# Block attention with a Fourier mixer and an MLP on one core: V and the next S in one step, q and k turned in separate steps

## The chip, the cores and the metric

The kernel runs on one core of a Trainium2 chip. The metric is the device time of one execution in microseconds (us). A core has five engines that run side by side, each working through its own instructions in order: TensorE (PE, matmuls and transposes into PSUM), VectorE (DVE), ScalarE (ACT), GpSimd (POOL) and SyncE (SP), which here mostly issues DMAs. They wait for each other by semaphores. PSUM holds what matmuls write, until VectorE or ScalarE has read it.

## What is computed

Attention within chunks of 64 tokens (8 batch elements, 8 heads, 576 tokens, head size 64), then per element a Fourier mix over tokens and features, a normalization and an MLP of width 2048, all in float32:

```python
scores = scale * np.matmul(q_c, k_c.transpose(0, 1, 2, 4, 3))
scores = scores - np.max(scores, axis=-1, keepdims=True)
attn = np.exp(scores)
attn = attn / (np.sum(attn, axis=-1, keepdims=True) + 1e-09)
out = np.matmul(attn, v_c)
...
mixed = np.real(np.fft.fft(np.fft.fft(x, axis=1), axis=2)).astype(np.float32)
u = x + mixed
un = (u - mu) / np.sqrt(var + 1e-06)
ch = np.maximum(un @ w_ch1, 0.0) @ w_ch2
return (u + ch).astype(np.float32)
```

The mix needs a whole batch element, so an element's attention must be finished before its mix, and its mix before its MLP.

## The kernel before

**Tiles.** An attention tile is two chunks of 64 tokens, that is 128 rows, of one element (kinds LO and HI), or the middle chunks of two elements (kind RE). Even elements have five tiles, odd ones four, 36 in all. MLP work is done in groups of four tiles; after those of the eight elements comes a ninth group with the RE tiles.

**One attention tile** goes through these parts:

- `att_T`: q and k are turned so that head features lie on partitions. From element 2 on (`n >= first[2]`) VectorE does it with one block transpose each for q and k (L333), both in the same step; for LO tiles POOL then copies one column of qT (L335). Then `load(n + 1)` issues the next tile's q and k on SP, four or eight DMAs each (L192), into single buffers, which must wait until the transposes have read them. In elements 0 and 1 TensorE transposes and ScalarE copies.
- `att_S`: 16 matmul calls of 64x64 write the scores `sc` (L365) into the one two-bank buffer of the pool `ps_a`. A float32 matmul call becomes two matmuls in the trace, so this is 32 of them.
- `softmax`: VectorE takes row maxima (L378) and subtracts them (L380), ScalarE does the exponential (L386), in place in `ex`.
- `att_P`: four 128x128 transposes of `ex` on TensorE (`turn`, L316, into a buffer of the pool `ps_t`, which has two buffers of one bank each), copied by ScalarE to `pT` (L393). These four are called T(ex) below.
- `att_V`: 16 calls of 64x65 (the 65th column of v is one, so that it gives the sum) write `xp` (L407), also into the buffer of `ps_a`. VectorE adds 1e-9, inverts and multiplies (L429 to L431) into `xall`. Then `load_v` issues a later tile's four v DMAs on SP, into a ring of three.

**The MLP.** For the first two groups the up product, and for the first group the down product, are plain loops of 512 columns. From then on both use a scheme with seven half-size products, numbered `o` = 0 to 6, of 128x256 matmuls. In the up product (`up_halves`) they are done for a pair of row blocks `r` = 0, 1; product `o` of one row block takes two calls, that is four matmuls. Each pair has two PSUM tiles per row block, `pa` (products 0, 1, 4) and `pb` (2, 3, 5, 6), and a matmul into such a tile waits until the last reader of that tile is done. Product 0 is copied by ScalarE (L979), product 1 is added by VectorE (L981), product 2 by VectorE (L983), product 3 by VectorE (L985). So product 1 waits for the copy of product 0, and product 3 for the addition of product 2 right before it, with only the other row block's four matmuls between them. In the down product (`down_halves`) a product of one row half takes sixteen matmuls, and the two halves alternate. The weights of the products come as slabs by DMA from memory (`fetch`, tiles `wa` and `wb`), issued on SP between the loads of q, k and v.

Before an MLP group its tiles are normalized (`normed`: for group 1 on ScalarE, L783, else VectorE, L785) and turned with four transposes each (`turned`, L316 again), called T(un) below, copied to `unT` by ScalarE (tiles 0 and 2, and all of the first two groups, L798) or VectorE (the others). They use the same two `ps_t` buffers. So do the Fourier products `z` (two at once, emptied by ScalarE) and `mix`.

**The order.** It is written by hand. `mlp(g)` yields after short pieces of work: in the plain loops after one row block, in `up_halves` after products 1, 3, 5 and 6, in `down_halves` after each product of a row half. After each yield the main loop calls steps of the next element's side work, `attention(b)`, three empty steps (`PAUSE`) and `fourier(b)`. `sizes` tells how many side steps an element has, and the loop spreads them evenly over the MLP pieces. In `attention` before, a tile has four steps: S with the softmax; the turning of the next tile; V of the tile before, with `ready` (which starts the exchange of rows, `shift`, and the sums, `fold`, on POOL); and T(ex). A first loop `attention_early` and `fourier_early` do element 0 with nothing beside it. Beside these, `round_weight` turns the float64 weights into float32 on VectorE and ScalarE in the first part of the run.

Of the kernel before, what the change touches and what calls it, by code (L numbers as in the profile page):

```python
# [16 lines left out]
def kernel(  # L17
# [153 lines left out]
        more_v[:, i * 2 * NJ * DV:(i + 1) * 2 * NJ * DV].rearrange("p (i j d) -> p i j d", i=2, j=NJ) for i in range(2)  # L171
    ]

    def load(n):

        for src, dst, nm, eng in ((q, qs, "q", nc.sync), (k, ks, "k", nc.scalar if n == 0 else nc.sync)):
            if n < first[1]:  # L180
                i = 2 * n + (nm == "k")
                t = start[:, (4 + i) * DM:(5 + i) * DM].rearrange("p (j r d) -> p j (r d)", r=2, d=D)
            else:
                t = one_p.tile([128, NJ, 4 * D], FP32, tag=nm, name=nm)
            if n >= first[2]:
                (b0, c0), (b1, c1) = chunks(n)
                parts = [(0, 32, b0, min(c0, c1))] if b0 == b1 else [(0, 16, b0, c0), (16, 16, b1, c1)]
                for g in range(4):
                    e, x0 = g // 2, g % 2 * 32
                    for r0, rows, b, c in parts:  # L190
                        from_ = src[b, e:H:2, c * CH:c * CH + 4 * rows, :].rearrange("j (p t) d -> p j (t d)", t=4)
                        eng.dma_start(  # L192
                            out=t[32 * g + r0:32 * g + r0 + rows, :, 0:4 * D - 32],
                            in_=from_[:, :, x0:x0 + 4 * D - 32],
                        )
                dst[n] = t
                continue
            t = t.rearrange("p j (r d) -> p (j r) d", d=D)[:, 0:H]
            (b0, c0), (b1, c1) = chunks(n)
            if b0 == b1 and c1 == c0 + 1:  # L200
                parts = [(0, 128, b0, c0)]
            else:
                parts = [(0, CH, b0, c0), (CH, CH, b1, c1)]
            for p0, np_, b, c in parts:
                eng.dma_start(
                    out=t[p0:p0 + np_], in_=src[b, :, c * CH:c * CH + np_, :].rearrange("h p d -> p h d")
                )
            dst[n] = t
# [72 lines left out]
            free.remove(fit[0])  # L281
            nc.sync.dma_start(out=raw(i).rearrange("p f r -> p (f r)"), in_=pieces[i][1].bitcast(U32))

    def round_weight(i):

        if i < len(pieces):
            w, t = pieces[i][0], raw(i)
            lo, hi, wi = t[:, :, 0], t[:, :, 1], w.bitcast(U32)
            p = power[i] = three_p.tile([128, 512], U32, tag="o", name="power")
            nc.vector.tensor_scalar(wi, hi, 0x000FFFFF, None, ALU.bitwise_and)
            nc.scalar.activation(out=w, in_=wi, func=ACTF.Copy, scale=2.0 ** -20, bias=1.0)
            nc.vector.tensor_scalar(p, hi, 0x7FF00000, None, ALU.bitwise_and)
            nc.scalar.activation(out=p, in_=p, func=ACTF.Relu, scale=-1.0, bias=top[:, 0:1])
            nc.scalar.activation(out=p, in_=p, func=ACTF.Relu, scale=-8.0, bias=top[:, 1:2])
        if 0 < i <= len(pieces):  # L300
            w, t = pieces[i - 1][0], raw(i - 1)
            lo, hi = t[:, :, 0], t[:, :, 1]
            p = power.pop(i - 1)
            nc.vector.scalar_tensor_tensor(w, lo, 2.0 ** -52, w, ALU.mult, ALU.add)
            nc.vector.scalar_tensor_tensor(p, hi, 0x80000000, p, ALU.bitwise_and, ALU.bitwise_or)
            nc.vector.tensor_tensor(out=w, in0=w, in1=p.bitcast(FP32), op=ALU.mult)
            r = raws.pop(i - 1)
            if i - 1 + len(spaces) < N_EARLY or r < N_LATE:
                free.append(r)
            load_weight(max(raws, default=i - 1) + 1)  # L310
# [6 lines left out]
        return pt  # L317


    def att_T(n):  # L320

        if n >= first[2]:
            for src, dst, nm in ((qs, qT, "qT"), (ks, kT, "kT")):
                a = src.pop(n).rearrange("p j (t b d) -> p j t b d", t=4, b=2)[:, :, :, 0]
                t = one_p.tile([128, NJ, 2, CH + 1], FP32, tag=nm, name=nm)
                low = kind(n) == LO and nm == "qT"
                to = t[:, :, :, CH:0:-1] if low else t[:, :, :, 0:CH]  # L330
                if kind(n) == HI:
                    to = to[:, :, ::-1]
                nc.vector.transpose(out=to.rearrange("p j c (r t) -> p j t c r", t=4), in_=a)  # L333
                if low:
                    nc.gpsimd.tensor_copy(t[:, :, :, 0:1], t[:, :, :, CH:CH + 1])  # L335
                dst[n] = t.rearrange("p j c t -> p (j c) t")
            if n + 1 < NT:
                load(n + 1)
            return
        a = qs.pop(n)  # L340
        pt = turn(lambda j: a[:, 2 * j:2 * j + 2, :].rearrange("p h d -> p (h d)"))
        t = one_p.tile([128, 2 * NJ, CH + 1], FP32, tag="qT", name="qT")
        low = kind(n) == LO
        nc.scalar.copy(t[:, :, CH:0:-1] if low else t[:, :, 0:CH], pt.rearrange("p j (c t) -> p (j c) t", c=2))
        if low and n < first[1]:
# [28 lines left out]
    def softmax(n):  # L374
        sc = scs.pop(n)
        s4 = sc[:, :, 0:NJ * CH].rearrange("p e (j k) -> p e j k", j=NJ)
        mx = sm_p.tile([128, 2, NJ], FP32, tag="mx", name="mx")
        nc.vector.tensor_reduce(out=mx, in_=s4, axis=AX.X, op=ALU.max)  # L378
        ex = two_p.tile([128, NJ, 2, CH], FP32, tag="ex", name="ex")
        nc.vector.tensor_tensor(  # L380
            out=ex.rearrange("p j e k -> p e j k"),
            in0=s4,
            in1=mx.unsqueeze(3).to_broadcast([128, 2, NJ, CH]),
            op=ALU.subtract,
        )
        nc.scalar.activation(out=ex, in_=ex, func=ACTF.Exp, scale=scale)  # L386
        es[n] = ex

    def att_P(n):
        ex = es.pop(n)  # L390
# [5 lines left out]
    def att_V(n):  # L396
        a, b = pT.pop(n), vs.pop(n)
        if n < first[1]:
            xp = early_xp
        else:  # L400
            xp = ps_a.tile([128, 2, 512], FP32, tag="att", name="xp")
            xp = [xp[:, e] for e in range(2)], xp
# [12 lines left out]
        xo = x[:, DM:0:-1] if kind(n) == HI else x[:, 0:DM]  # L415
        xo = xo.rearrange("p (j e d) -> p e j d", j=NJ, e=2)
        rd = sm_p.tile([128, 2, NJ], FP32, tag="rd", name="rd")
        if n < first[1]:
            for e in range(2):
                nc.vector.tensor_scalar_add(rd[:, e], xp[0][e][:, D:NJ * DV:DV], 1e-9)  # L420
            nc.vector.reciprocal(out=rd, in_=rd)
            for e in range(2):
                xe = xp[0][e][:, 0:NJ * DV].rearrange("p (j d) -> p j d", j=NJ)
                nc.vector.tensor_tensor(
                    out=xo[:, e], in0=xe[:, :, 0:D], in1=rd[:, e].unsqueeze(2).to_broadcast([128, NJ, D]), op=ALU.mult,
                )
# [79 lines left out]
    def attention_early():  # L506
# [32 lines left out]
        keep_warm(3)  # L539
        turn_tables()  # L540
        round_next()
        round_next()

    def attention(b):

# [10 lines left out]
                fold(b, NM)  # L556
            return kind(n) == HI

        if b < 2:
            att_T(lo)  # L560
            yield
        for n in range(lo, hi + 1):
            att_S(n)
            softmax(n)
            yield
            if n + 1 < NT and (b > 0 or n < hi):
                att_T(n + 1)
            yield
            if n > lo:
# [351 lines left out]
    def down_plain(g, h1):  # L921
# [4 lines left out]
        for m in range(KF):  # L926
# [15 lines left out]
                    store(n, o)  # L942
            for j in range(G):
                due = KF - (G - j + 1)
                if m == due - 1:
                    normed(g + 1, j)
                if m == due:
                    turned(g + 1, j)
# [125 lines left out]
    with tc.manual_schedule():  # L1074
# [26 lines left out]
            for _ in range(times):  # L1101
                nc.tensor.matmul(out=idle[:, 0:NQ], lhsT=warm[:, 0:128], rhs=warm[:, 0:NQ], start=True, stop=True)

        def round_next():
            nonlocal n_w
            if n_w <= len(pieces):
                round_weight(n_w)
                n_w += 1

        keep_warm(8)  # L1110
# [2 lines left out]
        for step, _ in enumerate(fourier_early()):  # L1113
            if step == 0:
                turn_dim_tables()
        round_next()
        PAUSE = 3

# [7 lines left out]
        sizes = []  # L1126
        for b in range(1, B):
            n_tiles = first[b + 1] - first[b]
            sizes.append(4 * n_tiles + PAUSE + 2 + NM + b % 2 + (b == 1))
        done, cur = 0, 0  # L1130
        begin = [0]
        for g in range(NG):
# [96 lines left out]
```

## Time and profile before

| What | us |
|---|---|
| median of 3 runs (1121.31 to 1125.09) | 1122.53 |
| the profiled execution, its own time | 1123.98 |
| span of its instructions | 1122.2 |
| matmuls of the scheme's down product with `h`, one row of the page (512, of `pa`) | 116.1 |
| all S matmuls (1152), busy | 25.0 |
| all V matmuls (`xp`, 992), busy | 21.6 |
| T(ex) (144) and T(un) (144), busy | 21.8 and 21.9 |
| block transposes of q and of k (27 each), busy | 29.8 and 29.4 |

The profile has a page (busy time of each engine, the time in slices, the costliest groups) and answers to questions about the trace. Three kinds of lines are used here. A *wait* line reads: engine, tile and line that waited, `<-` what ended the wait, then the total in us, how often, and the longest. A *timeline* line reads: start in us, duration in us, engine, line, operation, tile written `<-` tiles read, shape, how many instructions were merged into the line, and in brackets the engine's idle time before it with what ended it. A *groups* line has busy time and mean duration of all instructions of one kind. Matmuls overlap: the end of one is modelled and lies behind the start of the next, so the distance of starts tells what a matmul costs in a stream.

### The profile page before, as it was taken

How to read it: one execution, taken by the hardware profiler on the slowest of the kernel's cores; microseconds unless marked ns; L12 is line 12 of the kernel's file. 1: busy time of each engine (PE TensorE's matmuls, PEld its weight loads, DVE VectorE, ACT ScalarE, POOL GpSimd, SP SyncE). 2: the span in 40 equal slices, each digit the busy share in tenths (PEclk: the TensorE clock that was granted, in tenths of full speed). 3: DMA queues.
4: the chain of work that ended last, by engine and by line, in shares of the span. 5: the costliest groups of instructions: out<-in, count | busy, mean ns of one | idle time of the engine just before them, and what ended most of it. 6: DMA issues, size and time to landing. Idle time of an engine off the chain costs nothing. (4 is left out here: it accounts for less than half of the span.)

```text
span 1122.2 us, 18759 instructions
## 1 busy us (share of the span) xinstructions
PE 1090.6 (97%) x7042; PEld 845.3 (75%) x7042; DVE 571.0 (51%) x1206; ACT 298.3 (27%) x725; POOL 276.3 (25%) x403
## 2 busy tenths in 40 slices
PE   8899999999999999999999999899999999999998
PEld 6544454446888888788888888778888888888887
DVE  4799987332555365563555355635454434323521
ACT  4688443221112311322122212221132102201210
POOL 4200003235404240063105230154024400130130
PEclk9999999999999999999999999999999999999999
DMA  8777647678475536772567356853654346446332
GB/s 171 226 195 180 158 147 236 179 233 294 149 226 163 160 137 215 213 212 79 177 194 214 114 178 199 226 157 110 194 199 113 113 144 204 141 149 195 89 113 75
DMA packets 147969, 192.72 MB, mean 172 GB/s; under 512 B 66126, under 2 KB 104014, under 8 KB 140712
## 3 DMA queue, kind: packets, MB, share of 16 engines
q1 hardware_dynamic: 145768, 190.46, 56.1%
q8 instruction: 56, 0.92, 0.3%
q0 software_dynamic: 512, 0.68, 0.3%
q10 hardware_dynamic: 1600, 0.39, 0.2%
q14 instruction: 33, 0.27, 0.1%
HBM read 167.22 MB, written 24.12 MB: 171 GB/s over the span
## 5 line engine op out<-in xcount | busy, mean ns | idle before, releaser
L880 POOL TENSOR_TENSOR h<-h 128x256 f32<-128x256 f32 x64 | 55.5, 873 | 412.7 <-PE pb L974 303.5
L1021 PE MATMUL pa<-wb,h 128*128 128x256 f32 x512 | 116.1, 381 | 0.0
L1021 PE MATMUL pb<-wb,h 128*128 128x256 f32 x512 | 115.0, 381 | 0.0
L974 PE MATMUL pb<-unT,wa 128*128 128x256 f32 x448 | 106.6, 381 | 4.1 <-DVE wa L983 4.1
L974 PE MATMUL pb<-wa 128*128 128x256 f32 x448 | 107.3, 382 | 1.1 <-DMA wa<-s 1.1
L974 PE MATMUL pa<-unT,wa 128*128 128x256 f32 x448 | 107.8, 383 | 0.0
L1021 PEld LDWEIGHTS pa<-wb,h 128*128 128x128 f32 x512 | 95.8, 190 | 14.6 <-issue 1.6
L1021 PEld LDWEIGHTS pb<-wb,h 128*128 128x128 f32 x512 | 95.8, 190 | 12.9
L974 PEld LDWEIGHTS pb<-unT,wa 128*128 128x128 f32 x448 | 84.3, 190 | 18.3 <-DVE wa L983 6.8
L974 PEld LDWEIGHTS pb<-wa 128*128 128x128 f32 x448 | 83.4, 190 | 14.3 <-DVE wa L981 1.5
L974 PEld LDWEIGHTS pa<-unT,wa 128*128 128x128 f32 x448 | 83.2, 190 | 11.6
L989 ACT ACTIVATE h<-pa 128x256 f32<-128x256 f32 x56 | 21.5, 383 | 176.1 <-PE pa L974 143.1
L890 PE MATMUL up<-unT,wa 128*128 128x512 f32 x128 | 58.0, 599 | 2.4 <-ACT h L898 1.6
L981 DVE TENSOR_TENSOR wa<-pa,wa 128x256 f32<-128x256 f32 x56 | 23.8, 425 | 70.6 <-PE pa L974 70.6
L928 PE MATMUL dn<-wb,h 128*128 128x512 f32 x128 | 57.7, 599 | 1.3 <-ACT h L898 1.3
L1021 PE MATMUL pa<-wb,yall 128*128 128x256 f32 x256 | 58.2, 382 | 0.0
L974 PE MATMUL pa<-wa 128*128 128x256 f32 x224 | 54.1, 384 | 3.8 <-ACT wa L979 3.8
L907 PE MATMUL up<-unT,wa 128*128 128x512 f32 x128 | 57.5, 598 | 0.0
L1021 PE MATMUL pb<-wb,yall 128*128 128x256 f32 x256 | 57.1, 380 | 0.0
L1021 PE MATMUL pb<-wb 128*128 128x256 f32 x256 | 56.6, 379 | 0.0
L1021 PEld LDWEIGHTS pb<-wb 128*128 128x128 f32 x256 | 48.2, 190 | 6.3
L1021 PEld LDWEIGHTS pa<-wb,yall 128*128 128x128 f32 x256 | 47.7, 190 | 6.9 <-issue 0.5
(233 smaller groups left out, 1646.0 us busy)
## 6 DMA issues: line engine op xcount, KB each, us to landing
wb<-s SPq DMA_DIRECT2D x56, 1024.0 KB
wa<-s SPq DMA_DIRECT2D x196, 256.0 KB
xall<-in_moe_w_ch_dram SPq DMA_DIRECT2D x22, 512.0 KB
q<-in_q_dram SPq DMA_DIRECT2D x96, 112.0 KB
k<-in_k_dram SPq DMA_DIRECT2D x96, 112.0 KB
v<-in_v_dram SPq DMA_DIRECT2D x124, 64.0 KB
yall<-in_moe_w_ch_dram SPq DMA_DIRECT2D x10, 512.0 KB
s<-wb SPq DMA_DIRECT2D x20, 256.0 KB
```

The lines of the kernel that those rows point to most:

```text
L880: nc.gpsimd.tensor_tensor(out=h1[:, m, hi], in0=h1[:, m, lo], in1=h1[:, m, hi], op=ALU.subtract)
L890: nc.tensor.matmul(out=up, lhsT=w1[:, kk, m * 128:(m + 1) * 128], rhs=unT[:, kk], start=(kk == 0), stop=(kk == KD - 1),)
L907: nc.tensor.matmul(out=up, lhsT=w1[:, kk, m * 128:(m + 1) * 128], rhs=unT[:, kk], start=(kk == 0), stop=(kk == KD - 1),)
L928: nc.tensor.matmul(out=dn, lhsT=h1[:, m, s * 128:(s + 1) * 128], rhs=w2[:, m, :], start=(m == 0), stop=(m == KF - 1),)
L974: nc.tensor.matmul(out=dst, lhsT=w[:, kk, r], rhs=rhs[o][:, kk], start=(o in (0, 2) and kk == 0), stop=(kk == 1), skip_group_check=True,)
L981: nc.vector.tensor_tensor(out=b, in0=dst, in1=a, op=ALU.add)
L989: nc.scalar.activation(out=h1[:, m, lo], in_=dst, func=ACTF.Relu)
L1021: nc.tensor.matmul(out=dst, lhsT=lhs[:, m], rhs=w[:, m], start=(o in (0, 2) and m == 0), stop=(m == HF - 1), skip_group_check=True,)
```

## The change

- From element 2 on `attention` has three steps for a tile: the exponential, with turning and loading of the next tile's q; T(ex), with turning and loading of the next tile's k; V, directly followed by S and the softmax's VectorE part of the next tile, and only then `load_v`. The first tile's S is a step of its own. Element 1 keeps its four steps.
- The exponential is a function of its own, called one step after the subtraction.
- From element 2 on V writes into the two buffers of `ps_t`, and its sums and results are read one buffer at a time (five VectorE instructions in place of three).
- `sizes` counts three steps for a tile from element 2 on.
- In the plain down product `normed` of the next group's tiles is called one piece earlier.
- At the start, ScalarE's three operations on the second rounded weight piece are put off until after the copies of the first Fourier product of element 0.

```diff
-    def load(n):
+    def load(n, which="qk"):
         for src, dst, nm, eng in ((q, qs, "q", nc.sync), (k, ks, "k", nc.scalar if n == 0 else nc.sync)):
+            if nm not in which:
+                continue
...
-    def round_weight(i):
+    def round_weight(i, later=None):
...
+            def fraction(w=w, wi=wi):
+                nc.scalar.activation(out=w, in_=wi, func=ACTF.Copy, scale=2.0 ** -20, bias=1.0)
+
+            def exponent(p=p):
+                nc.scalar.activation(out=p, in_=p, func=ACTF.Relu, scale=-1.0, bias=top[:, 0:1])
+                nc.scalar.activation(out=p, in_=p, func=ACTF.Relu, scale=-8.0, bias=top[:, 1:2])
+
             nc.vector.tensor_scalar(wi, hi, 0x000FFFFF, None, ALU.bitwise_and)
-            nc.scalar.activation(out=w, in_=wi, func=ACTF.Copy, scale=2.0 ** -20, bias=1.0)
+            if later is None:
+                fraction()
             nc.vector.tensor_scalar(p, hi, 0x7FF00000, None, ALU.bitwise_and)
-            nc.scalar.activation(out=p, in_=p, func=ACTF.Relu, scale=-1.0, bias=top[:, 0:1])
-            nc.scalar.activation(out=p, in_=p, func=ACTF.Relu, scale=-8.0, bias=top[:, 1:2])
+            if later is None:
+                exponent()
+            else:
+                later += [fraction, exponent]
...
-    def att_T(n):
+    def att_T(n, which="qk"):
         if n >= first[2]:
             for src, dst, nm in ((qs, qT, "qT"), (ks, kT, "kT")):
+                if nm[0] not in which:
+                    continue
...
-                load(n + 1)
+                load(n + 1, which)
...
-        nc.scalar.activation(out=ex, in_=ex, func=ACTF.Exp, scale=scale)
         es[n] = ex
+        if n < first[2]:
+            exponential(n)
+
+    def exponential(n):
+        nc.scalar.activation(out=es[n], in_=es[n], func=ACTF.Exp, scale=scale)
...
             xp = early_xp
+        elif n >= first[2]:
+            xp = [ps_t.tile([128, 512], FP32, tag="pt", name="xp") for _ in range(2)], None
...
-        if n < first[1]:
+        if xp[1] is None:
...
-        round_next()
+        round_next(put_off)
...
-        if b < 2:
-            att_T(lo)
+        if b > 1:
+            att_S(lo)
+            softmax(lo)
             yield
+            for n in range(lo, hi + 1):
+                exponential(n)
+                if n + 1 < NT:
+                    att_T(n + 1, "q")
+                yield
+                att_P(n)
+                if n + 1 < NT:
+                    att_T(n + 1, "k")
+                yield
+                att_V(n)
+                if n < hi:
+                    att_S(n + 1)
+                    softmax(n + 1)
+                if n + 3 < NT:
+                    load_v(n + 3)
+                yield ready(n)
+            return
+        att_T(lo)
+        yield
...
-                if m == due - 1:
+                if m == due - 2:
                     normed(g + 1, j)
...
             if step == 0:
                 turn_dim_tables()
+                for do in put_off:
+                    do()
...
-            sizes.append(4 * n_tiles + PAUSE + 2 + NM + b % 2 + (b == 1))
+            sizes.append((4 * n_tiles + 1 if b == 1 else 3 * n_tiles + 1) + PAUSE + 2 + NM + b % 2)
```

More of the change, by code (lines that the diff above doesn't have):

```diff
@@ L565, in attention @@
             yield
-            if n + 1 < NT and (b > 0 or n < hi):
+            if n + 1 < NT:
                 att_T(n + 1)
@@ L1102, in keep_warm, with round_next @@
                 nc.tensor.matmul(out=idle[:, 0:NQ], lhsT=warm[:, 0:128], rhs=warm[:, 0:NQ], start=True, stop=True)
-        def round_next():
+        put_off = []
+        def round_next(later=None):
             nonlocal n_w
             if n_w <= len(pieces):
-                round_weight(n_w)
+                round_weight(n_w, later)
                 n_w += 1
```

## The prediction

> **What bounds the kernel now.** I read the page's busy shares first, then who waited for whom on TensorE, then the timeline where waits and short matmuls stand.
>
> ```profile
> span 1122.2 us, 18759 instructions
> ...
> PE 1090.6 (97%) x7042; PEld 845.3 (75%) x7042; DVE 571.0 (51%) x1206; ACT 298.3 (27%) x725; POOL 276.3 (25%) x403
> ```
>
> TensorE (PE) is busy 97% of the span at a granted clock of 0.999. So time is won only where PE does needless work or waits. The rows of its waits:
>
> ```profile
> PE pb L974 <- DVE wa L983: 4.1, 4, 1.0
> PE pa L974 <- ACT wa L979: 3.8, 7, 0.5
> ...
> PE pt L316 <- ACT un L783: 1.7, 1, 1.7
> ...
> PE z L604 <- POOL pm L495: 1.7, 1, 1.7
> ```
>
> Total, times, longest. A 128x256 matmul is drawn 0.38 us long, but in a stream the starts are 0.216 us apart (eight between 685.26 and 686.99); a row therefore shows some 0.16 us less than the time lost. I count from start to start. The same view shows a cost that no wait row has:
>
> ```profile
> 668.92 3.62 PE L1021 MATMUL pb<-wb,yall 128*128 128x256 f32 x16
> 672.47 0.70 PE L407 MATMUL xp<-v,pT 64*64 64x65 f32 x32
> 673.10 3.72 PE L1021 MATMUL pb<-wb,yall 128*128 128x256 f32 x16
> 676.66 0.60 PE L316 MATMUL pt<-ident,un 128*128 128x128 f32 x4
> ```
>
> Sixteen matmuls need 16 x 0.2158 = 3.45 us, yet the 64x64 block starts after 3.55 and the transposes after 3.56; the block's own step is 0.63. One block of 64x64 matmuls costs 0.093 + 0.63 + 0.104 = **0.823 us**; the 44 blocks after 290 us all give 0.822 to 0.824. Inside, the records start in groups of four, 0.058 apart (672.580, 672.638, 672.699), so eight groups are 0.467 us of work. The other 0.356 is going into the shape and out again.
>
> Two waits at a pair's start:
>
> ```profile
> 457.01 0.70 PE L365 MATMUL sc<-kT,qT 64*64 64x64 f32 x32
> ...
> 457.64 1.99 PE L974 MATMUL pa<-unT,wa 128*128 128x256 f32 x8
> 457.78 0.69 DVE L378 TENSOR_REDUCE mx<-sc 128x8 f32<-128x512 f32 x1 [0.23 <-PE sc L365]
> 458.50 0.69 DVE L380 TENSOR_TENSOR ex<-sc,mx 128x512 f32<-128x512 f32 x1
> 459.23 0.63 ACT L386 ACTIVATE ex<-ex 128x512 f32<-128x512 f32 x1 [1.02 <-DVE ex L380]
> 459.76 0.63 ACT L979 COPY wa<-pa 128x256 f32<-128x256 f32 x2
> 460.17 1.99 PE L974 MATMUL pa<-wa 128*128 128x256 f32 x8 [0.54 <-ACT wa L979]
> ...
> 462.00 1.89 PE L974 MATMUL pb<-wa 128*128 128x256 f32 x8
> ...
> 462.62 1.10 DVE L333 STREAM_TRANSPOSE qT<-q 128x512 f32<-128x512 f32 x1
> 463.56 1.06 DVE L333 STREAM_TRANSPOSE kT<-k 128x512 f32<-128x512 f32 x1
> 464.47 0.73 DVE L983 TENSOR_TENSOR wa<-pb,wa 128x256 f32<-128x256 f32 x2
> 464.93 1.99 PE L974 MATMUL pb<-unT,wa 128*128 128x256 f32 x8 [1.04 <-DVE wa L983]
> ```
>
> The exponential waits for VectorE (DVE), and the copy of product 0 behind it on ScalarE (ACT) holds product 1: late 0.70 us. Both block transposes stand ahead of product 2's addition, which holds product 3: due at 463.73, started 464.93, late 1.20.
>
> **The change, part by part** (minus is time won).
>
> *V and S in one block.* In the changed issue order 21 S blocks stand directly behind a V block: four for each even batch element from 2 on, three for each odd one. Each pair saves one way in and out: 21 x 0.356 = **-7.5**. A rule speaks against it. The Trainium skill, "TensorE: Matmul & The Clock Gate", in the part on the clock gate under "Wait — 56ns, not 53.3ns?", says that starts of matmuls never come closer than about 25 ns however small they are. By it, 32 matmuls are 0.80 us, the whole 0.823 is work, and the pairing saves nothing. The row decides: starts within a group are 5 to 7 ns apart and a matmul averages 14.6 ns. I take 7.5; zero is the far end.
>
> *Exponential one step later.* It no longer stands between S and product 0. All seven such waits go: 7 x 0.70 = **-4.9**. What follows it, T(ex), still has over two us after VectorE is done: S to T(ex) is at least 6.9 us of PE work, the chain V's reads, reduction, subtraction, exponential some 4.1.
>
> *Transposes and loads of q and k apart.* The four waits of 1.20 go. In six places (three each in elements 4 and 6) the q transpose alone stays between the additions of product 1 and product 2: 463.56, where it would end by these rows, + 0.46 (464.47 to 464.93) = 463.99 against 463.73 due, 0.26 each. -4.8 + 1.6 = **-3.2**. Each transpose issues four or eight 112 KB loads on SP; these now come in two bursts with slab loads (wa<-s) between, where one burst of k loads took 5.34 us at 340.53. Late slabs cost PE 1.4 us in two places; I leave them (0 to -1.4). POOL's copy of column 0 (0.20) moves along and has a step before S. The v loads now stand behind S, which SP does not wait for.
>
> *V's results in the two ps_t buffers.* In six places, once an element, the order is T(un) of the third normed tile, V, S. V's second buffer is the one that T(un) just filled, and it must first be copied by ACT. The nearest row is the last T(un) before the first MLP:
>
> ```profile
> 51.24 0.60 PE L316 MATMUL pt<-ident,un 128*128 128x128 f32 x4
> ...
> 52.51 3.70 PE L890 MATMUL up<-unT,wa 128*128 128x512 f32 x8 [0.67 <-ACT unT L798]
> ```
>
> The four transposes take 0.43, so PE is 0.84 late. V's first matmuls hide about 0.15: 6 x 0.7 = **+4.2** (0.5 to 1.2 each, the more if ACT is busy). Elsewhere the first buffer is long empty.
>
> *VectorE's burst.* V in two buffers gives five reads (the early tile at 28.08: 0.24 for two, 0.20, 0.76 for two), then 0.69 + 0.69 for S. By these starts, V's first matmul + 0.75 + 1.2 + 1.4, the burst ends 3.3 us after V's start, and PE's next dependent product can start at 3.3 + 0.46 = 3.76. Three pairs (elements 3, 5, 7) stand between products 1 and 2 of a pair, where product 3 is due 2.93 after V's start (1.29 - 0.09 + 1.73): 3 x 0.83 = **+2.5**; three lone V there, +0.15. The other 18 stand in the down product, where the other row half gives 3.45 us, or behind products 5 and 6. Here a second rule warns: the skill's "TensorEngine Tiling (Array Packing)", section "PSUM Bottleneck", says that packing speeds TensorE but not the emptying of PSUM, and to use both engines for it. Here VectorE alone empties V and S. By the rule every pair pays, 21 x 0.83 = +17.4; by the rows it is the three without slack.
>
> *Norm of the next tiles a step earlier in the first down product; steps 4n to 3n+1.* The transposes at 178.55 waited 1.9 for ACT's L783, queued behind an exponential. With S a step later and the norm one (3.6 us) earlier: **-1.9**. At 264.47 z waited 1.9 for POOL's fold; PE work between the last V and z grows from 14.3 to 17.9 us: **-1.9**. In odd elements z's halves move closer (1.7 us between); ACT empties both in about 1.3: 0.
>
> *Two rounding steps put off at the start.* ACT's 0.63 + 0.71 + 0.72 leave the queue ahead of z's copies. But VectorE's share of them starts at 40.06 anyway, so this gives 0.2. They now run after 42.66, ahead of the first rstd (44.02), to about 44.7. VectorE waits for that, and of 0.7 the later wait at 47.99 absorbs 0.3: **+0.4** (-0.2 to +0.7).
>
> Sum: -7.5 - 4.9 - 3.2 - 1.9 - 1.9 + 4.2 + 2.5 + 0.15 + 0.4 = **-12.2 us**. The profiled execution took 1123.98 us around its span of 1122.2, 1.45 above the median of 1122.53. It becomes 1111.8, the median **1110.4**.
>
> **Rivals.**
> 1. *New waits eat most of it.* ACT is busy at the six T(un), 1.2 each (+3.0), and the 18 other bursts cost 0.25 each (+4.5): 1118. For: V, S and two transposes make over 4 us of VectorE work per tile. Against: VectorE is 51% busy. 15%.
> 2. *No drain saved*, the issue floor rules or S waits for its own transposes: 1110.4 + 7.5 = 1118. Against: the 14.6 ns. 6%.
> 3. *Slower: every pair runs into VectorE.* Place: all 21. With one 0.42 addition already queued ahead, each costs 1.25: 26.3 instead of 2.5, so +11.6: 1134. It decides from a mean of 0.87 a pair, where the loss passes 3.4 us. Against: the 3.45 us of the down product. 5%.
>
> My forecast has 74%; its own range, from the ends above (slabs 1.4, burst 2.5, T(un) 1.2, start 0.6 below; T(un) 3, transposes 1.6, other bursts 2 above), is 1105 to 1117. Up to 1118 it takes in rivals 1 and 2 as worked out. No change is within 0.3% (1119.2 to 1125.9), about what these runs can tell apart. Faster: 0.74 and about two thirds of rivals 1 and 2, 0.87; same 0.08; slower 0.05.
>
> **What would show it.** In the profile after: V and S within one stretch of about 1.29 us; no wait of pa for ACT's wa; a new wait of xp for ACT's unT, six times; pb's waits for wa three times near 0.8 and six small; the waits at 178 and 264 gone; PE's busy time down by some 7. Wrong if a paired block still costs 1.65, if xp waits over 1 us each, or if PE waits for VectorE in the down product.

## The result, and the profile after

The changed kernel took 1115.60 us, the median of six runs (1114.57 to 1118.42); the kernel before, beside it, 1123.44 (1121.31 to 1125.66). The ratio is **0.9934**, 95% interval 0.9915 to 0.9952. By the medians 7.8 us were won. The profiled execution took 1115.22 us, against 1123.98 before: 8.8 us won, where the prediction added up 12.2. The time lies in the predicted range; the sum was 3.4 us too good.

The head of the page after, and rows of its view of TensorE's waits (microseconds in total, times, longest):

```profile
span 1113.4 us, 18823 instructions
...
PE 1085.2 (97%) x7042; PEld 848.6 (76%) x7042; DVE 582.7 (52%) x1260; ACT 297.7 (27%) x725; POOL 277.7 (25%) x403
```

```profile
PE pb L1017 <- DVE wa L1026: 3.7, 6, 1.2
PE xp L428 <- ACT unT L841: 2.5, 6, 0.4
PE pb L1017 <- DVE h L1034: 2.5, 3, 1.2
...
PE pa L1017 <- ACT wa L1022: 0.7, 2, 0.4
```

PE is busy 5.4 us less than before with as many matmuls (some 7 were expected). The first row holds the predicted waits of product 3, behind VectorE's burst (its five reads of V and two operations on S) and behind a q transposition. The second is the predicted wait of V behind T(un). The third, product 6 waiting for product 5's addition on VectorE, was not in the prediction. The last row shown stands where the seven waits behind the exponential stood; it has two places of another kind.

The timeline of one pair in element 3, PE, VectorE and the first of POOL's work:

```profile
337.09 0.70 PE L428 MATMUL xp<-v,pT 64*64 64x65 f32 x32
337.61 0.65 PE L380 MATMUL sc<-kT,qT 64*64 64x64 f32 x32
...
338.19 1.99 PE L1017 MATMUL pb<-wa 128*128 128x256 f32 x8
...
339.26 1.26 POOL L500 TENSOR_TENSOR sum<-xall 128x512 f32<-128x512 f32 x1 [0.18 <-POOL sum L499]
339.76 0.69 DVE L395 TENSOR_TENSOR ex<-sc,mx 128x512 f32<-128x512 f32 x1
340.37 0.74 DVE L1026 TENSOR_TENSOR wa<-pb,wa 128x256 f32<-128x256 f32 x2
...
340.83 1.99 PE L1017 MATMUL pb<-unT,wa 128*128 128x256 f32 x8 [0.65 <-DVE wa L1026]
...
342.00 0.43 DVE L1028 TENSOR_TENSOR h<-pb,wa 128x256 f32<-128x256 f32 x1 [0.89 <-PE pb L1017]
...
342.34 0.75 DVE L921 TENSOR_TENSOR wb<-h 128x256 f32<-128x256 f32 x1
...
345.09 0.98 DVE L922 TENSOR_TENSOR yall<-wb,h 128x256 f32<-128x256 f32 x1
345.86 1.97 POOL L522 TENSOR_TENSOR pm_rest<-two 64x128 f32<-64x128 f32 x4
346.00 1.07 DVE L348 STREAM_TRANSPOSE qT<-q 128x512 f32<-128x512 f32 x1
346.92 0.73 DVE L1034 TENSOR_TENSOR h<-pb,wa 128x256 f32<-128x256 f32 x2
...
347.38 1.35 PE L1017 MATMUL pb<-wa 128*128 128x256 f32 x5 [1.10 <-DVE h L1034]
```

V starts at 337.09, the burst ends at 340.4, product 3 starts 0.81 late (340.83). So far as predicted. With product 2's additions done at 341.1, VectorE has caught up: it stands idle for 0.89 us until product 3 is there (342.00). In the next five microseconds it falls behind again. The four operand operations of the down product (L921, L922), 0.42 us each where nothing disturbs them, take 0.75 to 0.98 while POOL runs its sums over the tile that has just been finished. A q transpose follows, the addition of product 5 comes behind that, and product 6 is 1.26 late.

From start to start, the terms are these (us; negative is time won against before). "Late" is the time from where the PE stream alone would have started a matmul to where it did.

| term | predicted | measured | where |
|---|---|---|---|
| V and S in one stretch | -7.5 | -7.1 | 15 blocks of 1.29, one of them 0.42 longer; 6 behind T(un) |
| exponential a step later | -4.9 | -3.8 | all seven gone (4.9); two others, 0.53 each |
| q and k transposes apart | -3.2 | -1.7 | 4.8 gone, six new ones of 0.28 to 1.35, 3.13 in all |
| V's second buffer behind T(un) | +4.2 | +4.4 | six blocks of 2.02 in place of 1.29 |
| burst before product 3 | +2.65 | +2.4 | 0.81, 0.82, 0.77 |
| product 6 behind VectorE's work after product 3 | none | +3.0 | 1.26, 1.36, 0.34 |
| first T(un) at 178, z at 264 | -3.8 | -3.8 | both waits gone |
| start, up to the first `up` | +0.4 | +1.0 | z began 1.2 later, behind its loads; from z to `up` -0.2 |
| slab waits | left out | -1.4 | both gone |

The measured column adds up to -7.0. Another 1.3 is that behind a wait or a short stall the second matmul starts 0.1 late too (nine such places fewer after the first T(un) of group 2) and that a wait of `up` at 70 us is 0.4 shorter; the remaining 0.4 or so of the 8.8 I can't place.

By batch element, from the first T(un) of one group to that of the next, a pattern shows that the terms hide. Before, the stretches with the attention of elements 3 to 7 take 119.70, 122.21, 119.48, 122.22, 118.68 us. After: 119.70, 119.30, 119.72, 120.02, 118.66. The odd elements gained nothing.

### The profile page after: what moved, and what is told of

Its sections match the earlier page's. It is cut to its first block, busy times and chain, and to the rows that moved or that the text cites. A ratio compares the mean times of both kernels' runs of the same rounds, so it can differ in the third digit from the quotient of the medians.

```text
span 1113.4 us, 18823 instructions
## 1 busy us (share of the span) xinstructions
PE 1085.2 (97%) x7042; PEld 848.6 (76%) x7042; DVE 582.7 (52%) x1260; ACT 297.7 (27%) x725; POOL 277.7 (25%) x403
## 5 line engine op out<-in xcount | busy, mean ns | idle before, releaser
L1064 PEld LDWEIGHTS pb<-wb,yall 128*128 128x128 f32 x256 | 48.2, 190 | 6.5
```

What stands on the lines that cost most here:

```text
L1064: nc.tensor.matmul(out=dst, lhsT=lhs[:, m], rhs=w[:, m], start=(o in (0, 2) and m == 0), stop=(m == HF - 1), skip_group_check=True,)
```

## The experiments

All times stand beside runs of the kernel before on the same chip (medians 1123.8 to 1124.3), so the ratios to it are compared. The changed kernel's is 0.9934 and its span 1113.4.

**1. V and S apart again, the rest of the change kept.**

```diff
                 att_V(n)
-                if n < hi:
-                    att_S(n + 1)
-                    softmax(n + 1)
                 if n + 3 < NT:
                     load_v(n + 3)
                 yield ready(n)
+                if n < hi:
+                    att_S(n + 1)
+                    softmax(n + 1)
+                    yield
```

The number of steps in an element follows (4n from element 2 on).

> The changed kernel with V and S in separate steps again (four steps a tile), all else kept. Both theories: each of the 21 blocks that were 1.29 us becomes two of 0.823, PE work +7.5 us. Theory A (the pairing pays for itself only partly: it brings the six waits of V for ACT's copy of T(un), 4.4 us, the three waits before product 3 behind V and S on VectorE, 2.4, and those before product 6, 3.0): most of these go, so the time stays within 3 us of the changed kernel, about 1114 to 1118. Theory B (the pairing is the gain, and the waits come from the transposes and the new step count): the waits stay and the time rises by about 7, to 1122.

1119.76 us, ratio 0.9961 (0.9948 to 0.9973), span 1117.5. From element 2 on 53 of its 54 blocks of V or S are 0.82 again (one V behind a T(un) takes 1.55), and no product 3 or 6 is over 0.15 late; three products 1 wait 0.39. So the shape does save 0.36 a pair, and the waits of both products come with the pairing and its places. But the elements are the finding: 3 to 7 take 118.28, 118.40, 118.27, 118.60 and 118.21 us, together **5.6 us less than with the pairs**. What the unpaired kernel loses lies up to the end of element 2's attention: from the first `up` to the first T(un) of group 2, where element 3's stretch begins, it takes 242.3 us, the changed kernel 233.1. There T(ex) waits 5.6 us once, since VectorE, with the softmax in its queue, stands 11.3 us for a transfer:

```profile
PE pt L329 <- ACT ex L406: 5.6, 1, 5.6
```

```profile
246.09 0.58 DVE L922 TENSOR_TENSOR wb<-h 128x256 f32<-128x256 f32 x1 [11.28 <-DMA s<-wb]
```

Behind this wait TensorE's granted clock is 0.50 until 253.7 (see the last section), which costs some 2 us more, and four pairs undone cost 1.4: together about the 9.2.

**2. V in ps_a, S in the two ps_t buffers.**

```diff
-        sc = ps_a.tile([128, 2, 512], FP32, tag="att", name="sc")
+        if n >= first[2]:
+            sc = [ps_t.tile([128, 512], FP32, tag="pt", name="sc") for _ in range(2)]
...
-        elif n >= first[2]:
-            xp = [ps_t.tile([128, 512], FP32, tag="pt", name="xp") for _ in range(2)], None
```

Softmax then takes two reductions and two subtractions of half the width.

> The changed kernel with the PSUM buffers exchanged: V writes into the buffer of ps_a, S into the two of ps_t. Theory A: V starts at once after T(un), and S, 0.5 us later, waits only for the rest of the copy, so the six blocks of 2.02 us become about 1.5: 3 us less, 1112.5. VectorE has the same number of reads, so the waits before products 3 and 6 stay. Rival: the wait only moves from V to S in full (blocks stay at 2.0), or scores in ps_t are read so late (after V's three reads) that the next T(un) or T(ex) waits: no gain, 1115.6 or more.

1118.35 us, ratio 0.9943 (0.9923 to 0.9963), span 1113.5. The six T(un)-V-S blocks shorten from 2.02 to 1.555: the wait is for T(un)'s buffer. But the first S of an element stands directly behind a T(un) as well, and now it waits in V's place:

```profile
PE sc L384 <- ACT unT L854: 2.1, 5, 0.4
```

Five blocks of 1.55 in place of 0.82, +3.6 against -2.8. The expectation had overlooked them.

**3. The exponential back behind the subtraction.**

```diff
         es[n] = ex
-        if n < first[2]:
-            exponential(n)
+        exponential(n)
```

and no call of it in the following step.

> The changed kernel with the exponential directly behind the subtraction again. Five pairs stand directly before a product 0. Theory A: ACT's copy of product 0 queues behind an exponential that waits for V's five reads and the softmax (3.3 us after V's start) and product 1 is late, now more than the 0.70 of before: with the copy of both row blocks some 1.6 us each, 5 times, +8 us, and the waits of pa for ACT's wa grow from 0.7 to about 8: 1123. Rival: the exponential was no matter with pairs, since V's and S's own matmuls cover it: within 2 us of the changed kernel.

1126.56 us, ratio 1.0019 (1.0012 to 1.0027), span 1123.3. The wait row of the page after (0.7, 2) has become

```profile
PE pa L1015 <- ACT wa L1020: 9.8, 9, 1.2
```

11.2 us from start to start. The exponential's later step is worth 10 us once V and S are paired, more than the 4.9 that it took away from the kernel before: with the burst ahead, it waits longer for VectorE and holds ScalarE's copies behind it for as long. Without this step the rest of the change comes out 0.2% behind the kernel before.

**4. q and k transposes and loads in one step.**

```diff
-                    att_T(n + 1, "q")
+                    att_T(n + 1)
                 yield
                 att_P(n)
-                if n + 1 < NT:
-                    att_T(n + 1, "k")
```

> The changed kernel with both block transposes and both loads in the exponential's step again. Theory A: in the six places of elements 4 and 6 between products 1 and 2 the k transpose adds about 1 us to the wait before product 3, and in elements 3, 5 and 7 it makes the wait before product 6 longer by about 1: +7 to +9 us, 1123 to 1125. Rival: the waits come from the loads being late and from POOL's sums beside VectorE rather than from the transposes' place: within 3 us.

1133.73 us, ratio 1.0091 (1.0067 to 1.0114), span 1131.4: 18 us more than the changed kernel, where 7 to 9 were expected. The timeline at the worst place:

```profile
347.23 1.08 DVE L348 STREAM_TRANSPOSE qT<-q 128x512 f32<-128x512 f32 x1 [1.09 <-DMA q<-in_q_dram]
...
350.95 1.08 DVE L348 STREAM_TRANSPOSE kT<-k 128x512 f32<-128x512 f32 x1 [2.63 <-DMA k<-in_k_dram]
...
351.88 0.73 DVE L1032 TENSOR_TENSOR h<-pb,wa 128x256 f32<-128x256 f32 x2
...
352.33 1.22 PE L1015 MATMUL pb<-wa 128*128 128x256 f32 x2 [5.77 <-DVE h L1032]
```

Both transposes were counted by their duration. Here they cost the wait for their loads: VectorE stands at the head of its queue for k's transfer with product 5's addition behind it, and product 6 comes 5.9 us late, in two elements. So the split does more than spread two transposes of 1.1 us: k's transpose stands a step later, behind product 5's addition, while its load lands at about the same time (here at 350.9; the k transpose of the changed kernel waits for it until 350.5, and no product waits behind it). Two slab waits of about 1.0 each and a halved clock behind the two long waits (some 1.6 us each, see the last section) are part of the 18 us as well.

**5. Pairs in element 2 only.** As experiment 1, with `and b == 2` for the pair and `and b > 2` for the lone S.

> V and S stay paired in element 2 (three steps a tile) and stand apart again from element 3 on (four steps a tile). Theory A (adding up the latenesses of each profile): from element 3 on the pairing costs more in waits for VectorE and in T(un)-V-S blocks than its drains save. In the wholly unpaired kernel the elements 3 to 7 took 118.28, 118.40, 118.27, 118.60 and 118.21 us where the changed kernel takes 119.70, 119.30, 119.72, 120.02 and 118.66, together 5.6 less, while its element 2 lost some 9. With each in its place: span 1113.4 - 5.6 = 1107.8, median about 1110, ratio 0.988; no product 3 or product 6 is late by over 0.2, and T(un)-V-S blocks of 2.02 remain only in element 2 (one). Theory B (the unpaired elements were short only because work had been left behind in its element 2, or their loads came earlier for it): the elements from 3 on take about 119.4 again, and the time is that of the changed kernel, 1115 to 1116.

1111.23 us, ratio **0.989** (0.9874 to 0.9907), span 1108.1 against 1107.8 worked out. Elements 3 to 7 take 118.62, 118.42, 118.26, 118.41 and 118.21. Product 3 is late once, by 0.27, product 6 nowhere. So theory A stands: with the places where the change puts them, the pairs of elements 3 to 7 cost more than they save. The terms come near: these elements hold 17 pairs, which save 17 x 0.356 = 6.1; they come with five T(un) blocks (5 x 0.73 = 3.7), product 3's 5.5 and product 6's 3.0, together 12.2, so 6.1 more than they save, where the five elements gain 5.5. Of product 3's 5.5, 3.1 stand behind q transposes and not behind a pair: with four steps a tile these fall into other places.

**6. As 2, but the first S of each element stays in ps_a** (`if n >= first[2] and n not in first`).

> V goes to ps_a and S to the two ps_t buffers, but the first S of each element, which stands directly behind T(un) 0, to ps_a. Theory A: with V in ps_a nothing stands between T(un) 2 and V, and S's second buffer, which T(un) 2 filled, is needed only one V block later: six blocks of 1.55 as in the run with all S in ps_t (0.26 each above a pair's 1.29, 1.6 together, where the changed kernel has 4.4), and the five first S blocks are 0.823 again (there 1.55, 3.6 together). Against the changed kernel -2.8, with the product 3 and product 6 latenesses (8.5) as they are: span about 1110.6, median about 1112.8, ratio 0.9905. Theory B (the buffers are not what the elements wait for: a later wait for VectorE takes up what an earlier one gives): the blocks shorten as said, but products 3 and 6 wait longer by as much, and the time stays at 1115.

1114.18 us, ratio 0.9917 (0.9902 to 0.9932), span 1112.0. The blocks are as A said: six of 1.55, five of 0.82, -2.8. But product 6 waits 3.7 in place of 3.0, and two pairs of element 2 are 1.93 and 2.09 long, where the changed kernel has 1.29 and 1.71: S waits there for the k transpose, whose load landed late. Half of the gain is left in the span, and the intervals overlap, so the gain is shown by the blocks, not by the time.

**7. No step of attention behind product 1.** In the products of a pair of row blocks, what is due there goes behind product 3, and at most one step goes into a place.

```diff
                 if o in (1, 3, 5, 6):
-                    yield h1
+                    yield "hold" if o == 1 else h1
...
-                    while done < due:
+                    while done < due and not isinstance(piece, str):
                         ...
                         done += 1
+                        if g >= first_of[1]:
+                            break
```

> In the products of the pairs of row blocks no step of attention stands between product 1 and product 2 any more; it goes behind product 3, and what is due there behind product 5. Theory A (product 3 is late because VectorE's burst or a q transpose stands ahead of product 2's addition): all nine latenesses of product 3 (2.40 + 3.13) go, and the burst no longer pushes product 5's addition, so product 6's 2.96 goes too. V now stands 1.7 us behind T(ex) in eight places, where ACT's copy of pT takes 0.6 and may be queued behind a relu: up to 0.3 each, +2. Sum -5.5 - 2.9 + 2 = about -6: span 1107, median 1109.5, ratio 0.988. Theory B (VectorE has too much work around these pairs in any order, the wait only moves): product 6 or V is late by what product 3 was, and the time stays within 1 us of 1115.

1111.47 us (1106.65 to 1113.71, the first of these the profiled execution), ratio **0.9882** (0.9856 to 0.9909), span 1104.9; this profile is thus of an execution 4.8 us below the median. Product 6 is late nowhere, product 1 neither; V, 1.7 us behind T(ex), doesn't wait. Product 3 is still late three times, 2.84 in all, but for another reason:

```profile
338.01 0.42 DVE L1026 TENSOR_TENSOR wa<-pb,wa 128x256 f32<-128x256 f32 x1 [0.44 <-PE pb L1017]
338.98 1.32 PE L1017 MATMUL pb<-unT,wa 128*128 128x256 f32 x5 [1.00 <-DMA wa<-s]
```

VectorE was done at 338.4; what comes late is the weight slab. (The third place, 0.65, ends with VectorE in the view; the half product that stands there had its addition done 0.9 us earlier, and experiment 11 shows that it is the slab too.) Its load is queued on SP behind the transfers that shift an element's rows, whose second half waits for the first to land:

```profile
331.38 0.59 SPq L482 DMA_DIRECT2D first<-xall  x1
334.03 1.10 SPq L484 DMA_DIRECT2D xall<-first  x2
335.17 0.55 SPq L485 DMA_DIRECT2D xall<-first  x1
335.82 1.95 SPq L912 DMA_DIRECT2D wa<-s  x4
```

So theory B falls: VectorE has time enough, and it is the place of the burst that costs. The wait that remains is a transfer that the pair had hidden: product 3 is due at 337.81 here and was due at 340.02 in the changed kernel, while the slab's load is issued only 1.0 earlier.

**8. POOL's sums one step later.** From element 2 on, `fold` is called in the step of T(ex) instead of that of V, S, except for an element's last tile.

> From element 2 on POOL's partial sums over a finished tile are issued one step later, in the step of T(ex) instead of that of V and S, so they no longer run beside VectorE's burst. Theory A (VectorE's operand operations took 0.75 to 0.98 us instead of 0.42 because POOL was running its sums beside them, and this is what made product 6 wait for product 5's addition): these operations behind the burst take 0.42 again, the two latenesses of product 6 of 1.26 and 1.36 fall below 0.3, about -2.3 us: span 1111, median 1113.3. Theory B (they are long for another reason, their operands or PE's traffic): they stay at 0.75 to 0.98, product 6 stays late, the time is that of the changed kernel or up to 2 more, since z then waits for the last sums.

1120.53 us (1116.14 to 1121.61), ratio 0.9954 (0.9933 to 0.9975), span 1114.3. As a whole no gain: z at 264 us now waits 3.5 us for the last sums. But the disputed operations answer. In the same place as in the changed kernel, with POOL's first sum now at 347.97:

```profile
345.18 0.42 DVE L927 TENSOR_TENSOR wb<-h 128x256 f32<-128x256 f32 x1
...
345.63 0.42 DVE L928 TENSOR_TENSOR yall<-wb,h 128x256 f32<-128x256 f32 x1
...
346.31 0.62 DVE L927 TENSOR_TENSOR wb<-h 128x256 f32<-128x256 f32 x1
...
346.96 0.42 DVE L928 TENSOR_TENSOR yall<-wb,h 128x256 f32<-128x256 f32 x1
347.07 0.90 POOL L929 TENSOR_TENSOR h<-h 128x256 f32<-128x256 f32 x1 [0.43 <-ACT h L1038]
...
348.24 1.11 DVE L348 STREAM_TRANSPOSE qT<-q 128x512 f32<-128x512 f32 x1 [0.85 <-DMA q<-in_q_dram]
```

Three of the four take 0.42; the fourth (346.31, 0.62) begins while POOL works on its own part of the operands. Product 6 is 0.70 and 0.52 late in place of 1.26 and 1.36, and that rest belongs to the q transpose, which now waits for its load. The third place, 0.34, is gone: it lies in the last element, which has no next q to turn. Theory A's mechanism stands, its time was spent elsewhere.

**9. The two small parts undone**: the two rounding steps at the start no longer put off, and the norm of the next tiles back to one step later.

> Two small parts of the change are undone in one kernel; they lie in different places and are read apart. At the start, ScalarE's share of the first two rounding steps stands ahead of z's copies again (the prediction put its being put off at +0.4, so undoing it would give 0.4 back: z to the first up 20.2 us; the two profiles, 20.82 before and 20.61 after, say it makes no difference or costs 0.2: 20.6 to 20.8). In the down products, the norm of the next tiles is issued one step later again. Theory A (the step earlier is what took the 1.9 us wait of the first T(un) at 178 away): the wait for ScalarE's un is back, +1.9, and the first T(un) of element 3 on is not later than in the changed kernel otherwise. Theory B (the wait went because the exponential moved, not the norm): no wait there, 0. By A the time is 1117 to 1117.5, by B that of the changed kernel, 1115.6; the spans by the two 1115 and 1113.4.

1116.89 us, ratio 0.9939 (0.9922 to 0.9955), span 1115.1. The wait of the first T(un) doesn't come back:

```profile
175.17 0.81 ACT L826 ACTIVATE un<-xall,shift,rstd 128x512 f32<-128x512 f32 x1
...
177.17 0.68 DVE L393 TENSOR_REDUCE mx<-sc 128x8 f32<-128x512 f32 x1
177.33 0.60 PE L329 MATMUL pt<-ident,un 128*128 128x128 f32 x4
...
179.79 0.61 ACT L406 ACTIVATE ex<-ex 128x512 f32<-128x512 f32 x1
```

`un` is finished at 176.0, and the exponential that once stood ahead of it comes at 179.79, since its S and its own step are later now. Theory B: with the later exponential, the norm's place costs nothing here. Where the 1.7 us of span come from is only partly seen (products 3 and 6 wait 0.9 more, one pair of element 2 waits 0.35 more). The put-off rounding can't be judged: the first `up` starts at 53.37 here and between 52.3 and 54.3 in the other kernels that have it put off, and here the clock was 0.50 for 3.4 us while z ran (last section), which the changed kernel's profile doesn't have.

**10. 6 and 7 together.**

> The run with the hold behind product 1 and that with the first S apart put together. The first left 12.1 us of T(un)-V-S blocks and 2.84 of slab waits, the second turned these blocks into 9.3 and left the rest. Theory A (the two act in different places and add): span 1104.9 - 2.8 = 1102.1, six blocks of 1.55, fifteen pairs of 1.29, the slab waits as they are. Theory B (the longer VectorE burst of S in two buffers, four operations of 0.37 in place of two of 0.69 with their waits, is paid somewhere, as in the run with the first S apart, where product 6 lost 0.7 more and the pairs 0.07 each): 1 to 1.5 of it comes back, span 1103 to 1104. Median by A about 1106, by B about 1107.

1107.68 us, ratio **0.9851** (0.9837 to 0.9866), span 1106.7. The T(un) blocks are 1.55, as in 6; two slab waits (2.5) remain, and two pairs of element 2 are 2.2 long, S waiting for a late load of k as in 6. By the profiles nothing is won over 7: its first `up` is 2.0 later and the rest 0.2 shorter. At most 1.6 of these 2.0 belong to the clock, which was 0.50 for 3.4 us at z here and not in 7. The medians differ by 3.8 us, but the intervals of the ratios overlap, and this stays open.

**11. As 10, with the row shift on POOL's queue** (`eng = nc.gpsimd` in `shift` for all elements).

> As the run before in this call, and the six small transfers that shift an element's rows (first<-xall and back) are issued by POOL instead of SP in all elements. In the run with the hold, product 3 waited for its slab in elements 3, 5 and 7 (1.17, 1.02, 0.65) because SP stood at the second half of this shift until the first had landed (2 us), and the slab loads stand behind it. Theory A: these three waits go, -2.8: span 1099.3, median about 1103, ratio 0.982; SP issues the slab loads some 4 us earlier there. Theory B (the slab loads are late for their buffer or for the DMA rings, not for SP's queue): they stay, or POOL's sums and z behind it come late by as much (POOL stands for 2 us where SP stood): within 0.5 us of the run before.

1103.69 us (1102.9 to 1104.31), ratio **0.9816** (0.9801 to 0.983), span 1101.5: the interval lies below that of 10 and far below the changed kernel's. All slab waits are gone. POOL now stands where SP stood, and the slabs leave at 330.7:

```profile
326.61 1.07 POOL L497 DMA_DIRECT2D xall<-first  x2 [3.89 <-DMA first<-xall]
...
330.73 2.91 SPq L925 DMA_DIRECT2D wa<-s  x4
```

Elements 3 to 7 take 116.97, 117.42, 116.99, 116.68 and 117.06 us. This version beats both kernels: 20 us below the one before, and by the ratios 13 below the changed one.

## Why the prediction came out as it did

The direction, the range and most steps held; the forecast of 1110.4 was 5.2 below the median of 1115.6. The profiled sum was 3.4 too good; the other 1.8 is the step from a profiled execution to a median, taken as -1.45 and measured as +0.4. That the sum came so near is partly luck: terms that cost more than forecast add up to 6.8 us, and against them stand the slabs' 1.4, which the sum had left out, and 1.8 of small delays and unplaced time.

- **Pairing, -7.5.** Right: pairs of 1.29 where two lone blocks take 1.65. The row decided rightly against the skill's floor of about 25 ns between starts. That the price of the shape is real doesn't make the pair a gain: experiment 5 wins 5 us by giving up 17 of the 21.
- **Exponential, -4.9.** The seven waits went. Beside that, two new ones of 0.53: product 6's relu waits on ScalarE for an addition behind the burst, with product 0's copy queued behind the relu. By experiment 3 the step is worth 10 in this kernel.
- **q and k, -3.2.** The price was mis-sized: 0.26 a place took VectorE as free and q as landed. Four of six are near it (0.28 to 0.38); one begins 0.16 after VectorE is free, for a reason that the trace doesn't show (0.53), and one waits for the load and costs 1.35:

```profile
713.91 1.11 DVE L348 STREAM_TRANSPOSE qT<-q 128x512 f32<-128x512 f32 x1 [0.98 <-DMA q<-in_q_dram]
714.86 0.74 DVE L1026 TENSOR_TENSOR wa<-pb,wa 128x256 f32<-128x256 f32 x2
...
715.33 1.35 PE L1017 MATMUL pb<-unT,wa 128*128 128x256 f32 x5 [1.19 <-DVE wa L1026]
```

- **V behind T(un), +4.2.** Right in place, number and size. In the timeline V's first matmuls run, then PE stands until ACT has emptied the second buffer:

```profile
302.58 0.60 PE L329 MATMUL pt<-ident,un 128*128 128x128 f32 x4
...
303.12 0.33 PE L428 MATMUL xp<-v,pT 64*64 64x65 f32 x4
303.22 0.58 ACT L841 COPY unT<-pt 128x512 f32<-128x512 f32 x1 [3.31 <-PE pt L329]
...
303.86 0.62 PE L428 MATMUL xp<-v,pT 64*64 64x65 f32 x26 [0.41 <-ACT unT L841]
```

- **Burst, +2.5, "the other 18 stand in the down product ... or behind products 5 and 6".** This is the step that failed. The price at product 3 was right to 0.1. But the three pairs were charged once, at the first product that depends on VectorE, and the second, product 6, was put at nothing (+3.0). The burst itself is not what it waits for: VectorE had emptied its queue in between. It waits for what comes next, the operand operations, made longer by the sums that V's end sets off on POOL, and the q transpose of elements 3 and 5, which the prediction priced in elements 4 and 6 only. Experiment 8 takes the two apart. Nor were the pairs behind product 5 free: two of them cause the 0.53 above. That POOL's sums lengthen these operations was visible before:

```profile
738.43 0.73 POOL L486 TENSOR_TENSOR two<-sum 128x256 f32<-128x256 f32 x1
738.60 0.83 DVE L878 TENSOR_TENSOR wb<-h 128x256 f32<-128x256 f32 x1
```

The Trainium skill states it, in "SBUF — State Buffer", section "Who interferes with whom": a VectorE instruction with two SBUF inputs contends with a GpSimd instruction that reads SBUF. The traces agree: in the place shown the operations with both inputs in SBUF go from 0.42 to 0.75-0.98, those with one in PSUM (L1028, 0.41 and 0.43) keep their time. They show in addition that it matters who begins: in 45 places of the changed kernel L922 begins before POOL's own operand operation, runs beside it and takes 0.42 or 0.43. The second rule that the prediction weighed, on the emptying of PSUM, wasn't borne out as a price for every pair: those of the down product have slack.
- **Norm earlier, -1.9.** The wait went, but experiment 9 shows that the later S and exponential are enough for that, without the norm's place.
- **z and sums, -1.9; slabs, "I leave them (0 to -1.4)".** The first right; the second came out at its far end.
- **Rivals.** None came as worked out. The first (new waits eat most of it) named ScalarE at T(un), which added nothing (0.73 each, as forecast), and the 18 other bursts, of which two cost 0.53 each. The second is refuted by the blocks of 1.29. The third, every pair running into VectorE, would need a mean of 0.87 a pair; measured is (2.4 + 3.0 + 1.1) / 21 = 0.31.

## What to carry to other kernels

When two steps are put behind each other to save an entry into another shape, follow the engine that drains both past the first dependent matmul, to the second: what else comes into its queue by then, what the end of the first step sets off on other engines, and what has to have landed for each instruction. Then choose the place before the pairing. Here the pairs of elements 3 to 7 lost 5.5 us against lone blocks in one set of places (experiment 5); with no step between products 1 and 2 (experiment 7) the same five stretches take 589.8 us in the profile, 2.2 less than the lone blocks, but the medians of the two runs are the same (1111.47 and 1111.23). Lone blocks with that rule were not run. And after a wait is gone, look at what it had hidden: the slab loads behind a waiting transfer were the next 4 us (experiment 11).

## What the runs showed of the hardware

A TensorE that stood 5.8 us didn't come back at full speed. In experiment 4 the view by stretches (busy time of each engine with the number of instructions, the granted clock, the DMA share and GB/s) reads, for the time after that wait and for the next:

```profile
352.30:355.60 3.30, 3.27 (x8) 2.65 (x9) 0.73 (x2) 1.37 (x3) 0.00 (x0) 0.50 1.01 283
355.60:360.00 4.40, 4.40 (x34) 3.51 (x36) 0.87 (x3) 1.75 (x4) 0.00 (x0) 0.99 1.10 233
```

At clock 0.50 eight matmuls start 0.43 apart instead of 0.216, and the wait costs 1.6 us beyond its length. The Trainium skill, "TensorE: Matmul & The Clock Gate", section "What's actually happening", has the clock halved after an idle window of about 3.4 us, which fits the 5.8. But the length of the wait alone doesn't decide. At z, after 2.4 us without a matmul, the clock of experiment 9 reads

```profile
31.80:35.20 3.40, 3.37 (x7) 2.51 (x8) 1.41 (x5) 1.96 (x3) 0.76 (x3) 0.50 0.89 304
```

and that of experiment 10 does the same after 2.7 us, while it stayed at 1.00 after the changed kernel's 2.4 us there, after 2.9 us in experiment 6 and after 3.3 us in experiment 8 (at 264). The stretches at 0.50 last 3.4 us in experiments 9 and 10, and 6.8 in 1 and 4, where they begin inside the wait. That would fit a clock that is decided for whole windows of 3.4 us, so that it counts how a wait lies in them; no run here tests that.
